# A planner's model of DMA: from one long hold of SyncE to a short issue and a turn on shared rings

## The chip, the cores and the metric

The kernel runs on one core of a Trainium2 chip. The metric is device time of one execution in microseconds (us): 921.68 us is the median of three runs before the change (920.78 to 922.54). A profile of one execution goes with it. TensorE is PE in its rows, with its weight loads as PEld; VectorE is DVE, ScalarE is ACT, GpSimd is POOL, SyncE is SP; SPq and ACTq are the queues on which SyncE and ScalarE issue DMAs.

## The reference

Attention with a threshold over 8 batches, 8 heads, 576 tokens and 64 dimensions a head, and behind it a gated convolutional feed-forward network, all float32:

```python
scores = scale * np.matmul(q, k.transpose(0, 1, 3, 2))
thresh = np.max(scores, axis=-1, keepdims=True) - tau
scores = np.where(scores >= thresh, scores, -1000000000.0)
scores = scores - np.max(scores, axis=-1, keepdims=True)
attn = np.exp(scores)
attn = attn / (np.sum(attn, axis=-1, keepdims=True) + 1e-09)
x = np.matmul(attn, v)      # heads side by side: 512 columns
h = np.maximum(x @ w_in, 0.0)                  # 512 -> 1024
conv_out = sum(conv_w[k] * hp[:, k:k + S, :] for k in range(3))
gate = 1.0 / (1.0 + np.exp(-conv_out))
out = h * gate @ w_out                          # 1024 -> 512
```

## The kernel before, in words

Each batch is cut into two chunks of query rows (256 and 320 of the 576), and each chunk is worked through for four pairs of heads. A **unit** is one tile of up to 128 query rows of one pair: the scores on PE (`ps_s`, line 571 in batch 0 and for the 64-row tile at the end of a batch, line 578 elsewhere), their maximum on DVE (L586), the exponential on ACT (L595), the mask on DVE (L598), small steps on `few` (L592, L615, L619, L622), and the division by the sum on POOL (L631). The masked weights `em` are turned by PE (`ps_t`, L690) and brought from PSUM into `eT` by ACT (L685). For 28 of the tiles the turning is done by DMA (function `cross`: a store of `parts` to `rows` at L663 and two transposing DMAs into `eT` at L668). When all tiles of a pair are turned, PE multiplies by V: first one step `mixed` on half blocks (L745), then four steps on whole ones (L754). The result `x` feeds the network: `mm1` (`ph`, L782), relu, three taps and gate on ACT and DVE (L797 to L819), a low half on POOL (L328), and `mm2` (`po`, L840), whose output goes out through `ot` (L847, L848).

In batches 1 to 7 keys and queries are split into a high and a low float32r half. `prep_k` loads `xk` (L521), scales it and takes the high half on ACT (L522, L523), takes the low half on POOL (L328), and then three DMAs from SBUF to SBUF put half-height pieces into `ks` (function `halves`, L511). `prep_q` does the same for a chunk's queries, with six such DMAs. `xk` has two buffers, which the 64-row tiles' keys (`k`, L485) use too, so that a batch's first `xk` load waits for PE to have read the second last `k` of the batch before.

Nothing of the order on the engines is written out by hand. The functions hand every operation to a planner (`Plan.op`) with its engine, a planned duration, what it reads and writes, and a rank less an `ahead`; `Plan.run` then steps through planned time, gives each free engine the ready operation of lowest rank, and emits the instructions in the order in which it picked them. On the chip each engine takes its own stream in that order, and a semaphore wait at its head holds all behind it. So a changed planned duration changes no work, only the order of the streams and, where an operation has a choice of engines (`other`: some steps on `few`, the division, low halves), the engine that does it. PE's rows fall in four kinds (`rows`, `cols`, `turn`, `full`, by how the 128x128 array is divided), with a planned cost for a change between kinds (`SWITCH`).

In the planner before, a DMA on SP holds SP for its whole planned transfer, 2.6 ns a column (`sp(n)`; half of that or 360 ns for the pieces of `halves`), and its data is there 2000 ns after that. The three first weight loads and the first keys, issued by ACT, hold ACT for 450 ns and have a latency of their own.

Of the kernel before, what the change touches and what calls it, by code (L numbers as in the profile page):

```python
# [22 lines left out]

LATENCY = {"pe": 210.0, "act": 145.0, "dve": 110.0, "pool": 75.0, "sp": 2000.0}

# [26 lines left out]
FAR = 3  # L52
EMS = 5

KEEP = {'rows': 2.304, 'cols': 1.613, 'turn': 3.226, 'full': 2.304}
# [30 lines left out]
class Plan:  # L86
# [12 lines left out]

    def op(self, engine, ns, fn, w=(), r=(), ahead=0.0, other=None, kind=None, late=0.0, port=False):  # L100
# [14 lines left out]
        for x in bufs:  # L115
            x.left += 1
        self.ops.append((((engine, ns), *(other or ())), self.rank - ahead, fn if other is not None else lambda e: fn(), before, bufs, kind, late, port))

    def run(self):
# [12 lines left out]
        live, turn = set(), {}  # L132
        last, port = "full", 0.0

# [20 lines left out]
        while events:  # L155
            t = events[0][0]
            while events and events[0][0] <= t:
                _, _, kind, x = heapq.heappop(events)
                if kind == "ready":
                    i, e = x  # L160
                    if taken[i] is None:
                        heapq.heappush(ready[e], (self.ops[i][1] + (0.0 if e == self.ops[i][0][0][0] else ALT), i))
                        if e == self.ops[i][0][0][0]:
                            load[e] += self.ops[i][0][0][1]
                elif kind == "release":
                    live.discard(x)
                    wake(x[0])
                elif kind == "done":
                    engine = taken[x]
                    for j in after[x]:  # L170
                        waits[j] -= 1
                        for e in came[j]:
                            late = 0.0 if e == engine == "pe" else LATENCY[engine] + self.ops[x][6] + (60.0 if e in ("pool", "pe") and e != engine else 0.0)
                            came[j][e] = max(came[j][e], t + late)
                        if not waits[j]:
                            offer(j)
                    for b in self.ops[x][4]:
                        b.left -= 1
                        if not b.left:
                            post(t + LATENCY[engine], "release", (b.tag, b.turn % b.bufs))  # L180
            for e in ready:
# [67 lines left out]
def tile_tau_attention_gated_ffn(  # L249
# [15 lines left out]
    P = 128  # L265
# [64 lines left out]

    def sp(n):
        return 2.6 * n

# [12 lines left out]
    def split(src, n, name, high, low, hr, lr, queue="sp"):  # L346
# [37 lines left out]
        if queue == "sp":  # L384
            op("sp", sp(2 * n), load, w=[hi, lo], ahead=w + AHEAD["load"])
        else:
            op("act", 450, load, w=[hi, lo], ahead=90, late=sp(2 * n) + LATENCY["sp"])
        op("act", act(n), f0, w=[a], r=[hi], ahead=w)
# [86 lines left out]
    def plain(b):  # L475
        return b == 0

    def prep_rows(i, b, p, o, w, tag):
# [5 lines left out]
        if i:  # L484
            op("sp", sp(S + D), lambda: nc.sync.dma_start(k[:], kp[b, p]), w=[(k, 0), (k, 1)], ahead=a + 2)  # L485
            op("sp", sp(2 * w), lambda: nc.sync.dma_start(q[:], qd[b, p, :, :, o:o + w]), w=[(q, 0), (q, 1)], ahead=a + 2)
        else:
            for j, on in enumerate((slice(0, CH), slice(CH, S + D))):
                op(
                    "act", 450, lambda on=on: nc.scalar.dma_start(k[:, on], kp[b, p, :, on]), w=[(k, j)], ahead=210 - 10 * j,  # L490
                    late=1500 + sp(CH) * (1 + j)
                )
                op(
                    "sp", sp(w) + 400, lambda j=j: nc.sync.dma_start(q[:, j], qd[b, p, :, j, o:o + w]), w=[(q, j)], ahead=210 - 10 * j
                )
        if w < P:
# [6 lines left out]
    def halves(dst, src, of, ahead):  # L503

        x, view, parts = src
        for part, head in of:
            j, half = part
            n = view.shape[-1]
            op(
                "sp", max(sp(n) / 2, 360),  # L510
                lambda j=j, half=half, head=head: nc.sync.dma_start(  # L511
                    dst[half * D:(half + 1) * D, j, :n].bitcast(F32), view[head * D:(head + 1) * D].bitcast(F32)
                ),
                w=[(dst, part)], r=[(x, parts[head])], ahead=ahead
            )

    def prep_k(b, p, ks):

        a = AHEAD["prep"]
        xk = plan.buf(wk, "xk", 2, [P, S + D], F32, f"xk_{b}_{p}")  # L520
        op("sp", sp(S), lambda: nc.sync.dma_start(xk[:, :S], kt[b, p]), w=[(xk, 0), (xk, 1)], ahead=a + 2)  # L521
        op("act", act(S), lambda: nc.scalar.activation(xk[:, :S], xk[:, :S], AF.Copy, scale=0.125), w=[(xk, 0), (xk, 1)], ahead=a)  # L522
# [8 lines left out]
    def prep_q(i, b, p, q1, q2):  # L531
# [3 lines left out]
        a = AHEAD["prep"]  # L535
        op("sp", sp(w), lambda: nc.sync.dma_start(xq[:], qt[b, p, :, o:o + w]), w=[(xq, 0)], ahead=a + 2)
        op("act", act(w), lambda: nc.scalar.activation(q1[:, 0], xq[:], AF.Copy), w=[(q1, (0, 0)), (q1, (0, 1))], r=[(xq, 0)], ahead=a)
# [104 lines left out]
    def crossed(i, t):  # L642
        c, p = pairs[i]
        return not plain(chunks[c].b) and p % 2 == 0 and t == order(i)[0]

    def cross(u, em, eT, off):
# [4 lines left out]
        for j in range(2):  # L651
# [9 lines left out]
            )  # L661
        op(
            "sp", sp(2 * S), lambda: nc.sync.dma_start(rows[:].rearrange("(q two) k -> q two k", two=2), parts[:]),  # L663
            w=[(rows, 0)], r=[(parts, 0), (parts, 1)], ahead=a
        )
        for j in range(2):
            def turn(j=j):
                nc.sync.dma_start_transpose(eT[:].bitcast(U16)[:, off // D + j], rows[j * P:(j + 1) * P, :])  # L668

            op("sp", 1350, turn, w=[(eT, (off, j))], r=[(rows, 0)], ahead=a, late=400)  # L670

# [159 lines left out]
    def mm2(m):  # L831
# [15 lines left out]
        op("act", act(DO, True), lambda: nc.scalar.activation(ot[:, :DO], po[:], AF.Copy), w=[(ot, 0)], r=[(po, 0)])  # L847
        op("sp", sp(DO), lambda: nc.sync.dma_start(tokens[m * P:(m + 1) * P, :], ot[:, :DO]), r=[(ot, 0)])  # L848

# [159 lines left out]
```

## Time and profile before

| | |
|---|---|
| median of three runs | 921.68 us (920.78 to 922.54) |
| the profiled execution | 923.11 us, of it 921.3 us span |
| instructions | 19164 |
| granted TensorE clock, mean | 0.992 |
| DVE, ACT, POOL busy | 767.0, 675.5, 600.6 us |
| moved by DMA | 137.02 MB, mean 149 GB/s |

The span runs from the first instruction to the last; times in rows are counted from its start. A row of a group gives the engine, the output and input tiles, the shape and the count, then the busy time and the mean of one in ns; behind the bar stands the idle time of the engine just before such instructions and what ended most of it. In the order of time a row gives the start, the length, and in square brackets the idle time before it with its releaser. Of the 1.8 us of the execution that lie around its span the profile shows nothing.

### The profile page before, as it was taken

How to read it: one execution, taken by the hardware profiler on the slowest of the kernel's cores; microseconds unless marked ns; L12 is line 12 of the kernel's file. 1: busy time of each engine (PE TensorE's matmuls, PEld its weight loads, DVE VectorE, ACT ScalarE, POOL GpSimd, SP SyncE). 2: the span in 40 equal slices, each digit the busy share in tenths (PEclk: the TensorE clock that was granted, in tenths of full speed). 3: DMA queues.
4: the chain of work that ended last, by engine and by line, in shares of the span. 5: the costliest groups of instructions: out<-in, count | busy, mean ns of one | idle time of the engine just before them, and what ended most of it. 6: DMA issues, size and time to landing. Idle time of an engine off the chain costs nothing. (4 is left out here: it accounts for less than half of the span.)

```text
span 921.3 us, 19164 instructions
## 1 busy us (share of the span) xinstructions
PE 880.3 (96%) x6056; PEld 706.7 (77%) x6056; DVE 767.0 (83%) x1859; ACT 675.5 (73%) x1455; POOL 600.6 (65%) x1043
## 2 busy tenths in 40 slices
PE   5888899998999999999999999999999999999998
PEld 2445668877788788888788787887778887887896
DVE  5987998978889889896989789896898878998543
ACT  5877787868778787787778687787767768787642
POOL 3664776857758677884767667685676748676422
PEclk9998999999999999999999999999999999999999
DMA  6644247467675576547665566556656377664000
GB/s 212 200 146 133 69 122 188 121 173 181 169 200 148 145 203 160 146 132 187 183 181 147 146 163 158 136 150 185 171 154 179 99 181 180 174 138 115 16 24 34
DMA packets 148260, 137.02 MB, mean 149 GB/s; under 512 B 85312, under 2 KB 116288, under 8 KB 148160
## 3 DMA queue, kind: packets, MB, share of 16 engines
q1 hardware_dynamic: 147296, 133.90, 54.4%
q10 hardware_dynamic: 864, 1.90, 0.6%
q8 instruction: 49, 0.80, 0.4%
q14 instruction: 51, 0.42, 0.2%
HBM read 58.88 MB, written 25.95 MB: 92 GB/s over the span
## 5 line engine op out<-in xcount | busy, mean ns | idle before, releaser
L631 POOL TENSOR_SCALAR em<-em,few 128x576 f32<-128x576 f32 x284 | 256.9, 912 | 35.2 <-DVE few L622 26.6
L595 ACT ACTIVATE em<-ps_s,few 128x576 f32<-128x576 f32 x288 | 209.7, 743 | 57.2 <-DVE few L586 53.3
L598 DVE SCALAR_TENSOR_TENSOR em<-ps_s,few,em 128x576 f32<-128x576 f32 x288 | 230.7, 812 | 25.0 <-ACT em L595 15.7
L782 PE MATMUL ph<-x,w1h 128*128 128x322 f32 (+1 forms) x1024 | 239.4, 305 | 2.9 <-ACT hp L797 2.8
L586 DVE TENSOR_REDUCE few<-ps_s 128x1 f32<-128x576 f32 x288 | 210.8, 749 | 35.5 <-PE ps_s L578 19.7
L685 ACT ACTIVATE eT<-ps_t 128x512 f32<-128x512 f32 (+2 forms) x360 | 169.7, 488 | 33.8 <-PE ps_t L690 31.6
L782 PEld LDWEIGHTS ph<-x,w1h 128*128 128x128 f32 x1024 | 174.3, 190 | 7.8 <-ACT hp L797 4.4
L690 PE MATMUL ps_t<-ident,em 128*128 128x128 f32 x1060 | 158.6, 279 | 11.2 <-POOL em L631 3.8
L578 PE MATMUL ps_s<-ks,q 128*128 128x288 f32 x896 | 155.2, 305 | 3.8 <-issue 1.0
L690 PEld LDWEIGHTS ps_t<-ident,em 128*128 128x128 f32 x1060 | 125.3, 142 | 39.6 <-POOL em L631 13.2
L782 PE MATMUL ph<-x,w1l 128*128 128x322 f32 (+1 forms) x512 | 151.3, 296 | 0.0
L578 PEld LDWEIGHTS ps_s<-ks,q 128*128 128x128 f32 x896 | 128.6, 188 | 21.1 <-issue 11.2
L328 POOL TENSOR_TENSOR gl<-t,gh 128x255 fp32r<-128x255 f32 (+9 forms) x192 | 121.0, 643 | 30.1 <-ACT gh L819 28.9
L754 PE MATMUL pa<-eT,v 128*64 128x320 f32 (+1 forms) x1024 | 133.1, 412 | 0.0
L840 PE MATMUL po<-w2h,gh 128*128 128x512 f32 x288 | 117.7, 409 | 2.4 <-ACT hp L797 2.4
L754 PEld LDWEIGHTS pa<-eT,v 128*64 128x64 f32 x1024 | 70.8, 138 | 59.1 <-issue 15.9
L840 PE MATMUL po<-w2l,gh 128*128 128x512 f32 x288 | 113.3, 393 | 0.0
L840 PE MATMUL po<-w2h,gl 128*128 128x512 f32 x288 | 113.1, 393 | 0.1
L804 DVE SCALAR_TENSOR_TENSOR t<-hp,cr 128x321 f32<-128x321 f32 (+1 forms) x128 | 85.3, 667 | 33.2 <-ACT hp L797 29.1
L782 PEld LDWEIGHTS ph<-x,w1l 128*128 128x128 f32 x512 | 96.9, 189 | 0.2
L811 ACT ACTIVATE t<-t,cm 128x321 f32<-128x321 f32 (+1 forms) x128 | 68.4, 536 | 25.2 <-DVE t L804 13.9
L809 DVE SCALAR_TENSOR_TENSOR t<-t,hp 128x321 f32<-128x321 f32 (+1 forms) x128 | 77.7, 607 | 10.6 <-ACT t L811 9.8
(82 smaller groups left out, 1109.2 us busy)
## 6 DMA issues: line engine op xcount, KB each, us to landing
q<-q SPq DMA_DIRECT2D x336, 64.0 KB, 2.1
v<-in_vc_dram SPq DMA_DIRECT2D x64, 288.0 KB, 3.6
rows<-parts SPq DMA_DIRECT2D x28, 576.0 KB, 3.7
k<-in_kp_dram SPq DMA_DIRECT2D x35, 320.0 KB, 3.5
out_dram<-ot SPq DMA_DIRECT2D x36, 256.0 KB, 2.3
xk<-in_kt_dram SPq DMA_DIRECT2D x28, 288.0 KB, 3.6
ks<-xk SPq DMA_DIRECT2D x56, 144.0 KB, 2.6
xq<-in_qt_dram SPq DMA_DIRECT2D x56, 128.0 KB, 2.4
```

The costliest lines, as they stand in the source:

```text
L328: engines[e].tensor_tensor(dst, x, y, op=ALU.subtract)
L578: nc.tensor.matmul(ps[:, c, :CH], lhsT=q[:, h, o:o + n], rhs=k[:, h, c * CH:(c + 1) * CH], start=(i == 0), stop=(i == 1))
L586: nc.vector.tensor_reduce(few[:rows, nm], ps[:rows, :, :CH], op=ALU.max, axis=mybir.AxisListType.XY, negate=True)
L595: nc.scalar.activation(view(), ps[:rows, :, :CH], AF.Exp, bias=few[:rows, nm])
L598: nc.vector.scalar_tensor_tensor(view(), ps[:rows, :, :CH], few[:rows, th], view(), op0=ALU.is_ge, op1=ALU.mult, accum_out=few[:rows, total])
L631: engines[e].tensor_scalar(sl, sl, by, to, op0=ALU.mult, op1=ALU.add)
L685: "act", act(w, True), lambda dst=dst, src=src: nc.scalar.activation(dst(), src(pt), AF.Copy),
L690: nc.tensor.transpose(out=pt[:, at:at + P], in_=em[:, int(b * P):int(b * P) + P], identity=ident[:])
L754: nc.tensor.matmul(pa[j * D:(j + 1) * D, :w], lhsT=vt[:, blk, :], rhs=eT[:, :w // D, blk, :], start=False, stop=(r == 3))
L782: nc.tensor.matmul(ph[:, :an], lhsT=w1[w][:, cb, fs], rhs=xs[cb][:, h, :an], start=(cb == 0 and i == 0), stop=(cb == NCB - 1 and i == 2))
L804: nc.vector.scalar_tensor_tensor(t[:, :kn], hp[:, k:kn + k], cr[:, j, f:f + 1], y, op0=ALU.mult, op1=ALU.add)
L840: nc.tensor.matmul(po[:], lhsT=x[:, f, at:at + P], rhs=w[:, f, :], start=(f == 0 and i == 0), stop=(f == NFB - 1 and i == 2))
```

## The change

Only what the planner believes of DMAs. A DMA holds its queue for an issue of 330, 460 or 560 ns. From 600 ns after the start of the issue it takes a turn on the rings, one after the other in the order of issue, for `rows * (n * 0.225 + 4) * 0.0737` ns (rows of n elements); 950 ns after its turn the data is there and the buffers it read are free. All DMAs, those of ACT too, go through a new helper `put`; the transposing ones hold SP for 1560 ns and the rings for 1785. `CROSS` names which of a pair's 128-row tiles are turned by DMA; with (1, 0) they are the same 28 as before. The 6517 operations that the planner gets are the same, with the same dependencies.

```diff
-LATENCY = {"pe": 210.0, "act": 145.0, "dve": 110.0, "pool": 75.0, "sp": 2000.0}
+LATENCY = {"pe": 210.0, "act": 145.0, "dve": 110.0, "pool": 75.0, "ring": 950.0}
...
-                            late = 0.0 if e == engine == "pe" else LATENCY[engine] + self.ops[x][6] + (60.0 if e in ("pool", "pe") and e != engine else 0.0)
+                            late = 0.0 if e == engine == "pe" else (LATENCY["ring"] if self.ops[x][8] else LATENCY[engine]) + self.ops[x][6] + (60.0 if e in ("pool", "pe") and e != engine else 0.0)
...
-                post(free[e], "done", pick)
+                if self.ops[pick][8]:
+                    ring = max(ring, t + 600.0) + self.ops[pick][8]
+                    post(ring, "done", pick)
+                else:
+                    post(free[e], "done", pick)
...
-    def sp(n):
-        return 2.6 * n
+    def put(n, fn, issue=460, rows=P, queue="sp", **kw):
+        op(queue, issue, fn, ring=rows * (n * 0.225 + 4) * 0.0737, **kw)
...
-            op("sp", sp(2 * n), load, w=[hi, lo], ahead=w + AHEAD["load"])
+            put(2 * n, load, issue=330, w=[hi, lo], ahead=w + AHEAD["load"])
...
-            op(
-                "sp", max(sp(n) / 2, 360),
-                lambda j=j, half=half, head=head: nc.sync.dma_start(
+            put(
+                n, lambda j=j, half=half, head=head: nc.sync.dma_start(
                     dst[half * D:(half + 1) * D, j, :n].bitcast(F32), view[head * D:(head + 1) * D].bitcast(F32)
-                ),
+                ), issue=560, rows=D,
...
-        op("sp", sp(S), lambda: nc.sync.dma_start(xk[:, :S], kt[b, p]), w=[(xk, 0), (xk, 1)], ahead=a + 2)
+        put(S, lambda: nc.sync.dma_start(xk[:, :S], kt[b, p]), w=[(xk, 0), (xk, 1)], ahead=a + 2)
...
-        op("sp", sp(NBLK * D), lambda: nc.sync.dma_start(vt[:], vc[b, p]), w=[(vt, 0)], ahead=AHEAD["prep"])
+        put(NBLK * D, lambda: nc.sync.dma_start(vt[:], vc[b, p]), w=[(vt, 0)], ahead=AHEAD["prep"])
...
-        return not plain(chunks[c].b) and p % 2 == 0 and t == order(i)[0]
+        return not plain(chunks[c].b) and t in [x for x in order(i) if TILES[x][1] == P][:CROSS[p % 2]]
...
-        op(
-            "sp", sp(2 * S), lambda: nc.sync.dma_start(rows[:].rearrange("(q two) k -> q two k", two=2), parts[:]),
-            w=[(rows, 0)], r=[(parts, 0), (parts, 1)], ahead=a
+        put(
+            864, lambda: nc.sync.dma_start(rows[:].rearrange("(q two) k -> q two k", two=2), parts[:]),
+            w=[(rows, 0)], r=[(parts, 0), (parts, 1)], ahead=a, late=-500
         )
...
-            op("sp", 1350, turn, w=[(eT, (off, j))], r=[(rows, 0)], ahead=a, late=400)
+            op("sp", 1560, turn, w=[(eT, (off, j))], r=[(rows, 0)], ahead=a, late=100, ring=1785)
```

Since the lines of the code shift by two at most places, L511 of before is L513 of the changed kernel, L521 is L523, L578 is L580, and so on.

The streams differ nearly everywhere, and mostly by a few places. The first place is SP at the start of batch 4, whose keys are `xk_4_0`, `xk_4_1` and `ks_4_0`, `ks_4_1` (batch, pair of heads); `q1_`, `q2_` are queries, `v_` values, `rows_`, `eT_` the turning by DMA, `ot_` the output. Before:

```order
L521 DMA xk_4_0_5476<-in_kt_dram 128x576
L511 DMA q1_32_5421<-q1_32_5421 64x256 x2
L511 DMA q2_32_5454<-q2_32_5454 64x256
L547 DMA v_30_5498<-in_vc_dram 128x576
L668 DMA_TRANSPOSE eT_30_5506<-rows_74_5423 128x9x128 x2
L547 DMA v_31_5558<-in_vc_dram 128x576
L511 DMA ks_4_0_5553<-ks_4_0_5553 64x576
L511 DMA ks_4_0_5553<-xk_4_0_5476 64x576
L511 DMA q1_32_5421<-q1_32_5421 64x256
L511 DMA q2_32_5454<-q2_32_5454 64x256
L521 DMA xk_4_1_5604<-in_kt_dram 128x576
L511 DMA ks_4_0_5553<-xk_4_0_5476 64x576
```

And in the changed kernel, on the same engine from the same load on:

```order
L523 DMA xk_4_0_5466<-in_kt_dram 128x576
L523 DMA xk_4_1_5471<-in_kt_dram 128x576
L493 DMA q_36_5476<-in_qd_dram 128x2x64
L493 DMA q_37_5482<-in_qd_dram 128x2x64
L549 DMA v_30_5509<-in_vc_dram 128x576
L670 DMA_TRANSPOSE eT_30_5517<-rows_74_5422 128x9x128 x2
L549 DMA v_31_5561<-in_vc_dram 128x576
L513 DMA ks_4_0_5526<-ks_4_0_5526 64x576
L513 DMA ks_4_0_5526<-xk_4_0_5466 64x576
L513 DMA ks_4_1_5577<-ks_4_1_5577 64x576
L513 DMA q1_33_5597<-q1_33_5597 64x256 x2
L513 DMA ks_4_0_5526<-xk_4_0_5466 64x576
```

The load of the second pair's keys, which had eleven DMAs between it and the first pair's, stands right behind it, and so do the loads `q_36`, `q_37` of the small tile's queries, which stood 20 places later; the last piece of `ks_4_0` stands behind the first piece of `ks_4_1`.

The second place is PE a little later in the same batch, where the scores `ps_s_80` are the first to use `ks_4_0`; `ph_6` is the network of an earlier chunk, `ps_t` the turning. Before:

```order
L690 MATMUL ps_t_78_4_5638<-ident_83,em_78_5528 128x128 x4
L782 MATMUL ph_6_0_5629<-x_26_4987,w1h_233 128x256
L782 MATMUL ph_6_0_5629<-x_26_4987,w1l_267 128x256
L782 MATMUL ph_6_0_5629<-x_26_4987,w1h_233 128x256
L782 MATMUL ph_6_0_5629<-x_27_5013,w1h_233 128x256
L782 MATMUL ph_6_0_5629<-x_27_5013,w1l_267 128x256
L782 MATMUL ph_6_0_5629<-x_27_5013,w1h_233 128x256
L690 MATMUL ps_t_79_0_5652<-ident_83,em_79_5574 128x128 x4
L690 MATMUL ps_t_79_4_5658<-ident_83,em_79_5574 128x128 x4
L782 MATMUL ph_6_1_5666<-x_24_4697,w1h_233 128x256
L782 MATMUL ph_6_1_5666<-x_24_4697,w1l_267 128x256
L782 MATMUL ph_6_1_5666<-x_24_4697,w1h_233 128x256
```

These rows end right ahead of `ps_s_80_0`. In the changed kernel PE has, from the same turning on:

```order
L692 MATMUL ps_t_78_4_5657<-ident_83,em_78_5551 128x128 x4
L580 MATMUL ps_s_80_0_5662<-ks_4_0_5526,q1_32_5385 128x288
L580 MATMUL ps_s_80_0_5662<-ks_4_0_5526,q2_32_5398 128x288
L580 MATMUL ps_s_80_0_5662<-ks_4_0_5526,q1_32_5385 128x288
L580 MATMUL ps_s_80_0_5662<-ks_4_0_5526,q2_32_5398 128x288
```

The eleven rows of `ph_6` and `ps_t_79` between the turning and the first use of `ks_4_0` (9 and 8 matmuls) now stand behind that use.

The third place is PE in batch 0, at the product with V of pair 2 (`pa_2`: one `mixed` step of line 745, then four steps of line 754), with the scores `ps_s_8` of a later tile. Before:

```order
L745 MATMUL pa_2_527<-eT_2_437,v_2_300 64x256 x2
L571 MATMUL ps_s_8_0_532<-k_4_383,q1_4_402 128x288 x2
L571 MATMUL ps_s_8_1_539<-k_4_383,q1_4_402 128x288 x2
L754 MATMUL pa_2_527<-eT_2_437,v_2_300 64x256 x8
L398 MATMUL pw_stage_4_560<-stage_4_f_487,ident_83 128x512
```

And in the changed kernel:

```order
L747 MATMUL pa_2_474<-eT_2_405,v_2_277 64x256 x2
L756 MATMUL pa_2_474<-eT_2_405,v_2_277 64x256 x8
L405 MATMUL pw_stage_3_500<-stage_3_f_364,ident_83 128x512
L406 MATMUL pw_stage_3_500<-w1h_275,minus_126 128x512
L692 MATMUL ps_t_6_0_530<-ident_83,em_6_431 128x128 x4
```

The scores no longer part the product's steps. Over the program 25 of the 36 `mixed` steps were followed at once by the steps of their own product, and now 34 are; the changes to and from the `rows` and `cols` kinds number 157 before and 142 after, 57 of them in the first 200 planned PE operations of either kernel.

More of the change, by code (lines that the diff above doesn't have):

```diff
@@ L98, in buf, with op @@
         return b
-    def op(self, engine, ns, fn, w=(), r=(), ahead=0.0, other=None, kind=None, late=0.0, port=False):
+    def op(self, engine, ns, fn, w=(), r=(), ahead=0.0, other=None, kind=None, late=0.0, port=False, ring=0.0):
         i = len(self.ops)
@@ L116, in op @@
             x.left += 1
-        self.ops.append((((engine, ns), *(other or ())), self.rank - ahead, fn if other is not None else lambda e: fn(), before, bufs, kind, late, port))
+        self.ops.append((((engine, ns), *(other or ())), self.rank - ahead, fn if other is not None else lambda e: fn(), before, bufs, kind, late, port, ring))
     def run(self):
@@ L384, in split @@
         if queue == "sp":
[L385 removed]
+            put(2 * n, load, issue=330, w=[hi, lo], ahead=w + AHEAD["load"])
         else:
[L387 removed]
+            put(2 * n, load, issue=330, queue="act", w=[hi, lo], ahead=90)
         op("act", act(n), f0, w=[a], r=[hi], ahead=w)
```

23 lines of the change are left out of this document (10 added, 13 removed).

## The prediction

> **What bounds the kernel now.** I read the page's busy times and clock first, then the stretches, then PE's rows in order of time for the idle time in them.
>
> ```profile
> span 921.3 us, 19164 instructions
> PE 880.3 (96%) x6056; PEld 706.7 (77%) x6056; DVE 767.0 (83%) x1859; ACT 675.5 (73%) x1455; POOL 600.6 (65%) x1043
> ```
>
> PE is the bound: 880.3 of 921.3 us, so 41.0 us of idle time is all that another order can win, apart from work that PE does less of. The stretches say where it lies (start and end, then busy time of PE, PEld, DVE, ACT, POOL, the granted clock, the DMA engines' share, GB/s):
>
> ```profile
> 0.00:50.00 50.00, 36.61 (x188) 19.37 (x190) 39.14 (x107) 32.82 (x66) 24.46 (x55) 0.97 0.61 190
> 50.00:100.00 50.00, 44.87 (x268) 26.39 (x265) 41.23 (x93) 38.93 (x79) 29.40 (x43) 0.93 0.42 128
> 100.00:150.00 50.00, 44.40 (x295) 34.77 (x294) 47.42 (x105) 40.91 (x86) 35.94 (x56) 0.97 0.54 133
> 150.00:200.00 50.00, 49.89 (x347) 41.22 (x347) 41.86 (x106) 36.76 (x80) 34.81 (x67) 1.00 0.57 157
> ...
> 200.00:250.00 50.00, 47.39 (x344) 37.23 (x343) 45.67 (x108) 39.12 (x84) 35.37 (x57) 1.00 0.66 170
> ```
>
> The first 150 us hold 13.4, 5.1 and 5.6 us of the 41.0; everything behind them holds 16.9. The DMA engines are little more than half busy. So transfers as such bound nothing; what counts is when a wanted one lands, and what an order puts in front of PE.
>
> **The change part by part.** It alters no instruction's work. It alters order, and I cost four effects of that.
>
> (1) Changes between PE's kinds. The rows of the chain that ended last (start, length) show the matmuls right behind a product with V and the same ones elsewhere:
>
> ```profile
> 738.90 4.46 PE pa L754 x32
> 743.36 0.58 PE ps_t L690 x4
> ...
> 788.94 3.60 PE pa L754 x32
> 792.54 1.25 PE ps_s L578 x8
> ...
> 805.27 1.07 PE ps_s L578 x8
> ...
> 809.21 0.59 PE pa L745 x8
> 809.80 1.26 PE ps_s L578 x8
> ...
> 817.77 0.44 PE ps_t L690 x4
> ```
>
> A change costs 0.58 - 0.44 = 0.14 us (turning) to 1.26 - 1.07 = 0.19 us (scores). The order has 157 of them before and 142 after, and the first 200 planned operations, where PE is not the bound, have 57 in either, so the 15 saved lie behind them. 15 x 0.14 to 0.19 = 2.1 to 2.9 us; I take **-2.3**, nearer the turning, which follows such a product more often. Nothing hides it: it is PE's own time in stretches where PE is over 97% busy.
>
> (2) Loads for a new batch that come too late. PE's rows with an idle time in brackets, and ACT's row behind the first of them:
>
> ```profile
> 226.18 0.39 PE L782 MATMUL ph<-x,w1h 128*128 128x256 f32 x1 [2.08 <-ACT hp L797]
> 441.01 0.76 PE L578 MATMUL ps_s<-ks,q 128*128 128x288 f32 x4 [0.89 <-DMA ks<-xk]
> 654.90 0.77 PE L578 MATMUL ps_s<-ks,q 128*128 128x288 f32 x4 [1.05 <-issue]
> ```
>
> ```profile
> 227.47 0.31 ACT L497 ACTIVATE q<-q 128x128 f32<-128x128 f32 x1 [1.34 <-DMA q<-in_qd_dram]
> ```
>
> 441.01 and 654.90 are the first uses of a batch's second pair of keys, whose load moves up to stand behind the first pair's (the front's SP rows for batch 4). At 226.18 PE waits for ACT. ACT's next gap there, 1.34 us, is for a small query load, which moves 12 to 20 places up SP. The sum is 0.89 + 1.05 + 1.34 = 3.28; with the loads 6 us and more earlier I take it all, **-3.3**. Bounds: nothing, if ACT or DVE is next late, and -4.0, with 2.08 for 1.34.
>
> (3) The first keys of a batch. Here the change works against PE. SP's rows in batch 4, then PE's first use of these keys, then issue to landing (KB each, median us):
>
> ```profile
> 413.66 0.68 SPq L521 DMA_DIRECT2D xk<-in_kt_dram  x1
> ...
> 417.04 3.41 SPq L668 DMA_TRANSPOSE eT<-rows  x2
> ...
> 423.50 0.47 SPq L511 DMA_DIRECT2D ks<-ks  x1
> ...
> 427.50 0.46 SPq L511 DMA_DIRECT2D ks<-xk  x1
> ```
>
> ```profile
> 431.77 1.22 PE L578 MATMUL ps_s<-ks,q 128*128 128x288 f32 x8
> ```
>
> ```profile
> xk<-in_kt_dram SPq DMA_DIRECT2D x28, 288.0 KB, 3.6
> ks<-xk SPq DMA_DIRECT2D x56, 144.0 KB, 2.6
> ```
>
> The last piece is issued at 427.50, lands at about 430.1, and is used at 431.77: 1.7 us to spare. In the new order the use moves ahead of 9 matmuls of `ph` and 8 of `ps_t`. Their lengths are in these rows:
>
> ```profile
> 695.21 0.87 PE ps_t L690 x8
> ...
> 713.93 1.34 PE ph L782 x9
> ```
>
> That is 2.2 us, so the use would be 0.5 us too early if the last piece leaves SP when it did. It may leave 2.0 us earlier (right behind its sister at 425.02 plus an issue: no loss), or 1.0 us later, since it now stands behind a piece that waits for ACT and behind two query pieces of about half a microsecond each (1.5 us lost). I take 0.5, the middle and the one that changes SP least, and the same in batches 2, 3 and 5 to 7, where the first use moves by 2 to 28 places of the plan: 6 x 0.5 = **+3.0**, bounds 0 and +9.0. Batch 1 I leave out: there the first use moves 7 places back. What waits behind such a stall is all of PE's stream, so nothing hides it.
>
> (4) Batch 0. PE's rows again:
>
> ```profile
> 43.09 0.65 PE L745 MATMUL pa<-eT,v 64*64 64x256 f32 x4 [0.58 <-ACT eT L685]
> 46.81 0.78 PE L571 MATMUL ps_s<-k,q 64*128 64x288 f32 x2 [3.07 <-ACT q L500]
> ```
>
> ```profile
> 25.03 1.95 PE L754 MATMUL pa<-eT,v 128*64 128x256 f32 x16
> ```
>
> PE had begun `pa_2`, then waited 3.07 us for the queries of `ps_s_8`, while the 16 ready matmuls of `pa_2`, 1.95 us long, stood behind (the front's third place). Now they stand ahead and fill that much: **-2.0**. Against it: DVE is busy for 39.1 of these 50 us and does no less work, so PE may just wait later (bound 0). For more: the gap may go entirely (-3.1). The weight pieces come a few places later in every stream; the network's first use of them stands at the same PE place, and I cost this at nothing, covered by the attention work put ahead; without that cover it is about one piece on PE, 0.5 to 1 us.
>
> The clock is the open item here. It is granted at 0.97, 0.93 and 0.97 in the first three stretches, 50 x (0.03 + 0.07 + 0.03) = 6.5 us of full speed, and at 1.00 behind 150 us even where PE pauses for 2.08 us. If the loss comes from the head's idle time, filling it returns a part. I put nothing in the sum and keep up to -4 us as a bound.
>
> The Trainium skill ("TensorE: Matmul & The Clock Gate", section "HAM oscillation — how this bites in real kernels") has it that only idle gaps of TensorE over some 3.4 us cost clock. No gap behind the start is that long here, so by it the sum would stay as it is and the bound of -4 would be empty; the row of 0.93 in a stretch whose waits are shorter than that speaks against it, and the row decides.
>
> DMA issues themselves, 774 on SP, are as many as before. The choice of an engine for a small step moves 7 limits and 7 guards more to DVE, each like this row's:
>
> ```profile
> L592 DVE TENSOR_SCALAR few<-few,ntau 128x1 f32<-128x1 f32 x163 | 30.8, 208 | 0.8
> ```
>
> That is 14 x 0.21 = 2.9 us of DVE, hidden under PE, which is 113 us busier over the span.
>
> The **sum**: -2.3 - 3.3 + 3.0 - 2.0 = -4.6 us. The profiled execution took 923.11 us, 1.4 us over the median of the three; from it 918.5, and by the median of the runs **917.1 us**.
>
> **The rivals.** *Late keys (slower).* The planner now believes that keys are there earlier than the rows say. For `xk` it plans 600 + 128 x (576 x 0.225 + 4) x 0.0737 + 950 = 2.8 us against 3.6, for a piece of `ks` 600 + 630 + 950 = 2.2 against 2.6: 1.2 us a batch over the two steps. Also its plan never lets SP stand in front of a wait, while the real one does:
>
> ```profile
> SPq L848 <- ACT ot L847: 91.6, 19, 24.3
> SPq L511 <- ACT q L537: 46.7, 21, 5.9
> ```
>
> That is 138 us in which whatever stands behind on SP waits too. With the upper price of 1.5 us and the same again at the second keys, six batches lose 6 x 3.0 = 18.0; without the -3.3 and the -2.0, and with the -2.3, that is +15.7, or 937. The milder form is the first keys alone at 1.5: 9.0 - 2.3 = +6.7, or 928.4. It is slower than now as soon as a batch loses over (2.3 + 3.3 + 2.0) / 6 = 1.3 us. For it: planned landings are short. Against it: the K loads themselves start earlier and two at a time.
>
> *Idle time only moves.* PE waits mostly for a unit's chain on DVE, ACT and POOL, and DVE is 83% busy. If each pause that goes comes back a few units on, and the saved changes of kind end as waits, the time stays at 921.7. For it: the streams meet again at the same sets of PE operations at many points, so gains in between must show as idle time somewhere. Against it: in the stretches behind 150 us PE has no such reserve of idle time.
>
> *The clock and the bursts too.* Earlier attention work leaves the network's matmuls as filler for DVE's crowded moments. Then of the 16.9 us of idle time behind 150 us another 4 go, with the clock's 4: 917.1 - 8 = 909.
>
> *The order is as before.* That the change does nothing is excluded by the front's rows.
>
> **How the numbers follow.** The forecast, a gain of 2 to 8 us, 0.45; clock and bursts 0.12; only moved 0.21; late keys 0.22. Faster by over 0.2% (below 919.8, about what a measurement of this kernel can tell from no change): nearly all of the first two, 0.57. Within 0.2%: 0.20. Slower: 0.23. The range leaves out one in ten on each side: down to 910, near the clock case, and up to 925, half way into the milder late keys. The forecast's own range is 913 to 920.
>
> **What would show it.** (1) Groups L690 and L578 on PE with a lower mean, PE's busy time 2 us lower. (2) Two `xk` loads back to back at each batch's start, and no PE gap of about 1 us at the second keys. (3) Gaps of 0.5 us, and not 1.5, at the first use of `ks` in batches 2 to 7. (4) The 3.07 us gap near 47 us down to about 1, with the clock of the first stretches as the open item. The prediction is wrong if PE's idle time stays near 41 us, or if PE gaps released by DMA or by ACT's `xk` rows sum to more than 8 us.

## The result, and the profile after

| | before | after |
|---|---|---|
| median of four runs each, taken side by side | 921.57 us (920.78 to 922.54) | 913.67 us (912.62 to 914.90) |
| ratio, 95% interval | | 0.9914 (0.9897 to 0.9932) |
| the profiled execution, of it span | 923.11, 921.3 us | 912.62, 910.8 us |
| granted TensorE clock, mean | 0.992 | 0.993 |

The change makes the kernel 7.9 us faster. The two profiled executions lie 10.5 us apart, because the one of before took longer than its median and the one of after is the shortest of its four. So differences between the two traces are about 2.6 us too large in sum. The span and PE's line on the page of after:

```profile
span 910.8 us, 19147 instructions
PE 874.6 (96%) x6056; PEld 708.6 (78%) x6056; DVE 751.2 (82%) x1871; ACT 673.8 (74%) x1459; POOL 603.5 (66%) x1027
```

PE is busy 5.7 us less than before (880.3) and idle for 36.2 us instead of 41.0. The stretches of after, with the columns of the prediction's:

```profile
0.00:50.00 50.00, 37.08 (x202) 20.37 (x202) 37.80 (x102) 33.77 (x69) 22.73 (x47) 1.00 0.60 194
50.00:100.00 50.00, 44.28 (x263) 27.23 (x264) 43.02 (x93) 38.29 (x78) 33.46 (x48) 0.93 0.41 128
100.00:150.00 50.00, 42.94 (x277) 32.14 (x277) 46.17 (x115) 40.55 (x85) 37.79 (x58) 0.93 0.54 146
150.00:200.00 50.00, 50.00 (x373) 41.86 (x374) 47.65 (x122) 40.36 (x90) 39.09 (x69) 1.00 0.60 152
200.00:250.00 50.00, 49.69 (x357) 41.07 (x350) 43.04 (x111) 40.46 (x84) 34.91 (x52) 1.00 0.79 198
```

The first 150 us now hold 12.9 + 5.7 + 7.1 = 25.7 us of idle time, 1.6 more than before. Behind them are 36.2 - 25.7 = 10.5, 6.4 less than before's 16.9. The difference of the two traces is therefore -5.7 (PE's busy time) + 1.6 (the first 150 us) - 6.4 (the rest) = -10.5 us. Nothing is won at the start, where most of the idle time is.

In batch 4 after the change, the loads of the first two pairs of keys, ACT's splitting of the second pair, the last piece of `ks_4_1`, and its first use on PE:

```profile
409.96 0.92 SPq L523 DMA_DIRECT2D xk<-in_kt_dram  x2
...
415.95 0.67 ACT L524 ACTIVATE xk<-xk 128x576 f32<-128x576 f32 x1
419.52 0.69 ACT L525 ACTIVATE ks<-xk 128x576 fp32r<-128x576 f32 x1
...
424.86 0.46 SPq L513 DMA_DIRECT2D ks<-xk  x1
...
432.53 0.77 PE L580 MATMUL ps_s<-ks,q 128*128 128x288 f32 x4
```

The gap of 0.89 us at this use (441.01 before) is gone, and the last piece starts on SP 7.7 us ahead of the use. ACT's two steps on the second pair stood much later before:

```profile
430.76 0.68 ACT L522 ACTIVATE xk<-xk 128x576 f32<-128x576 f32 x1
432.57 0.69 ACT L523 ACTIVATE ks<-xk 128x576 fp32r<-128x576 f32 x1
```

The load moved by 17 us (426.82 before), and ACT's second step by 13. Some 4 us of each is the trace's own lead at this place (the batch's first load leaves at 409.96 instead of 413.66). Which of the two moves matters is decided by the experiments `early_keys` and `late_keys`.

At the start, SP's second queries and the two loads of V, ACT's step on the first queries, and PE:

```profile
2.17 0.68 SPq L493 DMA_DIRECT2D q<-in_qd_dram  x1
2.90 1.48 SPq L549 DMA_DIRECT2D v<-in_vc_dram  x2
...
5.98 0.72 ACT L503 ACTIVATE q<-q 128x256 f32<-128x256 f32 x2 [2.82 <-DMA q<-in_qd_dram]
...
6.45 2.46 PE L573 MATMUL ps_s<-k,q 64*128 64x288 f32 x8 [6.45 <-ACT q L503]
...
52.14 1.33 PE L573 MATMUL ps_s<-k,q 64*128 64x288 f32 x4 [4.63 <-DVE em L600]
```

PE's first row before:

```profile
4.53 1.33 PE L571 MATMUL ps_s<-k,q 64*128 64x288 f32 x4 [4.53 <-ACT q L500]
```

PE starts at 6.45 us instead of 4.53. Three more loads are under way when the first queries come in, and ACT waits 2.82 us for queries. The gap of 3.07 us at 46.81 is gone, but a gap of 4.63 us, released by DVE, stands at 52.14. In the trace fifteen small steps on the convolution's weights (L454) hold DVE from 45.86 to 49.31, ahead of the maximum that this chain needs, and steps on a piece of the network's weights (L383, L386) hold it from 49.90 to 51.26, ahead of the mask.

### The profile page after: what moved, and what is told of

It is laid out like the page before. It is cut to its first block, busy times and chain, and to the rows that moved or that the text cites. A ratio compares the mean times of both kernels' runs of the same rounds, so it can differ in the third digit from the quotient of the medians.

```text
span 910.8 us, 19147 instructions
## 1 busy us (share of the span) xinstructions
PE 874.6 (96%) x6056; PEld 708.6 (78%) x6056; DVE 751.2 (82%) x1871; ACT 673.8 (74%) x1459; POOL 603.5 (66%) x1027
## 4 chain that ended last, share of the span: by engine, by line
PE 73%; ACT 8%; DVE 6%; POOL 5%; DMA 4%; issue 3%; SPq 2%; ACTq 0%; POOLq 0%; DVEq 0%
PE po L842 20%; PE ph L784 16%; PE pa L756 12%; PE ps_s L580 11%; PE ps_t L692 9%; PE ps_s L573 3%; ACT em L597 2%; POOL em L633 2%; DVE em L600 2%; ACT eT L687 2%; PE pa L747 2%; DVE few L588 2%; DMA q<-in_qd_dram 1%; SPq L513 1%; DMA q<-q 1%
## 5 line engine op out<-in xcount | busy, mean ns | idle before, releaser
L633 POOL TENSOR_SCALAR em<-em,few 128x576 f32<-128x576 f32 x287 | 262.8, 924 | 29.9 <-DVE few L624 22.1
L784 PE MATMUL ph<-x,w1h 128*128 128x322 f32 (+1 forms) x1024 | 233.7, 304 | 0.6 <-ACT hp L799 0.5
L580 PE MATMUL ps_s<-ks,q 128*128 128x288 f32 x896 | 156.8, 306 | 5.3 <-DMA q<-q 2.1
L580 PEld LDWEIGHTS ps_s<-ks,q 128*128 128x128 f32 x896 | 129.2, 189 | 20.2 <-issue 8.2
L806 DVE SCALAR_TENSOR_TENSOR t<-hp,cr 128x321 f32<-128x321 f32 (+1 forms) x128 | 75.6, 594 | 28.0 <-ACT hp L799 28.0
L813 ACT ACTIVATE t<-t,cm 128x321 f32<-128x321 f32 (+1 forms) x128 | 68.0, 535 | 25.2 <-DVE t L806 12.2
L811 DVE SCALAR_TENSOR_TENSOR t<-t,hp 128x321 f32<-128x321 f32 (+1 forms) x128 | 73.1, 573 | 11.4 <-ACT t L813 9.8
```

The source lines that it names most:

```text
L580: nc.tensor.matmul(ps[:, c, :CH], lhsT=q[:, h, o:o + n], rhs=k[:, h, c * CH:(c + 1) * CH], start=(i == 0), stop=(i == 1))
L633: engines[e].tensor_scalar(sl, sl, by, to, op0=ALU.mult, op1=ALU.add)
L784: nc.tensor.matmul(ph[:, :an], lhsT=w1[w][:, cb, fs], rhs=xs[cb][:, h, :an], start=(cb == 0 and i == 0), stop=(cb == NCB - 1 and i == 2))
L806: nc.vector.scalar_tensor_tensor(t[:, :kn], hp[:, k:kn + k], cr[:, j, f:f + 1], y, op0=ALU.mult, op1=ALU.add)
```

## The experiments

Three explanations were weighed. The first is that the gain is the forecast's terms: loads that come earlier, and fewer changes of kind on PE. The second is that it comes from one part of the new model, either the short issue or the rings, or from one part of the program. The third is that any new order moves the time by several us, and this one is a good draw. Three sets of four kernels were run, each beside runs of the kernel before. "Idle" is the span less PE's busy time on the page; "changes" are the planned changes of kind behind the first 200 planned PE operations. The runs of before spread from 920 to 928 us, most of them near the lower end; the ratio weighs all runs and can differ from the quotient of the medians by some 2 us.

| kernel | median (runs) | ratio, 95% interval | PE busy, idle | changes |
|---|---|---|---|---|
| before, the three sessions | 921.96, 921.94, 922.92 | 1 | 880.3, 41.0 | 100 |
| after, from the result | 913.67 (4) | 0.9914 (0.9897 to 0.9932) | 874.6, 36.2 | 85 |
| `ring_late` | 919.48 (8) | 0.9962 (0.9936 to 0.9988) | 877.4, 39.8 | 90 |
| `ring_early` | 928.12 (10) | 1.0047 (1.0028 to 1.0066) | 885.1, 43.3 | 100 |
| `long_hold` | 931.08 (5) | 1.0079 (1.0052 to 1.0106) | 885.2, 44.5 | 109 |
| `short_hold` | 942.12 (4) | 1.0198 (1.0159 to 1.0237) | 883.0, 57.8 | 93 |
| `old_1950` | 928.25 (5) | 1.0081 (1.0063 to 1.0099) | 880.9, 41.9 | 101 |
| `old_2050` | 921.67 (9) | 0.9993 (0.9977 to 1.0008) | 882.9, 37.3 | 105 |
| `new_925` | 920.33 (9) | 0.9976 (0.9955 to 0.9998) | 876.8, 40.7 | 86 |
| `new_975` | 922.33 (9) | 0.9990 (0.9971 to 1.0009) | 879.5, 41.4 | 99 |
| `new_again` | 915.16 (6) | 0.9910 (0.9883 to 0.9937) | 874.9, 40.9 | 85 |
| `early_keys` | 921.73 (12) | 0.9990 (0.9970 to 1.0009) | 882.2, 38.9 | 100 |
| `late_keys` | 960.60 (6) | 1.0400 (1.0368 to 1.0431) | 882.7, 76.0 | 85 |
| `old_start` | 920.23 (12) | 0.9971 (0.9954 to 0.9989) | 872.6, 43.6 | 85 |

### One part of the program, one part of the model

`ring_late` plans with the old model through batch 0 and with the new one from the loads of batch 1 on; `ring_early` is the other way round (`rank < 17`). The transposing DMAs follow the same switch.

```diff
+RINGS = lambda rank: rank >= 17
...
-        op(queue, issue, fn, ring=rows * (n * 0.225 + 4) * 0.0737, **kw)
+        if RINGS(plan.rank):
+            op(queue, issue, fn, ring=rows * (n * 0.225 + 4) * 0.0737, **kw)
+        elif queue == "sp":
+            kw.pop("late", 0)
+            op("sp", old or max(2.6 * n * rows / P, floor), fn, **kw)
+        else:
+            op("act", 450, fn, late=slow, **kw)
```

> The planner's old model of DMA for everything up to batch 0, the new one from the loads of batch 1 on. Theory A (the gain lies behind batch 0, where the idle time of PE went from 12.3 to 4.6 us and its own work from 757.3 to 752.7 us): 911 to 915 us, with the first matmul back at about 4.5 us. Theory B (the gain is made in the first hundred us, by the reordered start): 919 to 922. Theory C (any reshuffling of the streams moves the time by several us either way): anything from 912 to 925.

> The new model up to batch 0, the old one from the loads of batch 1 on. Theory A: 919 to 923 us, no faster than before. Theory B: 912 to 916. Theory C: anything from 912 to 925.

In the third and the fourth kernel the whole program has one half of the new model. `long_hold` holds SP as long as before, and the data comes by the rings. `short_hold` has the short issue, and the data comes when the old model says, without rings.

```diff
+        hold = old or max(2.6 * n * rows / P, floor)
+        op(queue, hold if queue == "sp" else issue, fn, ring=rows * (n * 0.225 + 4) * 0.0737, **kw)
```

```diff
+        if queue == "sp":
+            hold = old or max(2.6 * n * rows / P, floor)
+            op("sp", issue, fn, late=hold - issue, **kw)
+        else:
+            op("act", 450, fn, late=slow, **kw)
```

> SP held for the whole planned transfer as before, but the data there by the rings' turn and 950 ns. Theory A in its form A1 (what counts is that SP is planned free at once, so that a batch's loads stand back to back): 919 to 924 us. In its form A2 (what counts is the earlier planned landing, which puts attention ahead): 912 to 916.

> SP held for the issue alone as in the change, but the data there when the old model had it (hold and 2000 ns), no rings. A1: 912 to 916 us. A2: 919 to 923.

By the medians, the new model behind batch 0 alone wins 2.5 us, and in batch 0 alone it loses 6.2 (3.5 and 4.3 by the ratios). Together they win 7.9, so the parts do not add. The halves of the model add even less: one half costs 9.1 us, the other 20.2, and both together win 7.9. That batch 0 gains nothing fits the stretches above. No single part can be given the gain; what made `short_hold` as slow as it is was not looked into further.

### A constant that means nothing to the chip

A planned latency was moved by 25 or 50 ns (2.5%), in the old model and in the new one. No operation or dependency changes on the chip, only the order and, with it, the engine of a few small steps (DVE has 1871 instructions in after and 1877 in `new_925`). The other three kernels differ in the number alone.

```diff
-LATENCY = {"pe": 210.0, "act": 145.0, "dve": 110.0, "pool": 75.0, "ring": 950.0}
+LATENCY = {"pe": 210.0, "act": 145.0, "dve": 110.0, "pool": 75.0, "ring": 925.0}
```

> The changed kernel with 925 ns after the rings' turn in place of 950; PE operations 0.7 places from the change, 143 changes of kind against 142. A: 912 to 916. C: farther off.

> The same with 975 ns: PE operations 3.0 places from the change, and 161 changes of kind against 142, as many as before the change. A: 912 to 917. If the saved changes of kind are most of PE's 4.6 us less work: 2 to 3 us above the change, 916 to 918. C: anything from 912 to 925.

> The kernel before with the planned latency of a DMA at 1950 ns in place of 2000. It means nothing for the machine and moves a PE operation by 2.1 places in the mean. If a reshuffling alone moves the time (theory C), by several us: below 918 or above 925. If the model counts (A): 919.5 to 923.5.

> The same with 2050 ns; PE operations 2.3 places from before. C: below 918 or above 925. A: 919.5 to 923.5.

The third explanation holds to a large part. 25 ns in either direction take back 6 and 8 of the 8 us, and 50 ns off the old constant cost 6.3, while 50 ns on top of it change nothing that can be told (0.9993). The three orders of the new model have medians of 913.7, 920.3 and 922.3 (mean 918.8), the three of the old one 921.6, 928.3 and 921.7 (mean 923.8). With some 8 us between orders of one model, the 5.0 us between the means are suggested by three orders each, not shown.

### The same order, with one thing moved

For the last four kernels the order on every engine was written into the kernel as a list, so that one engine's stream could be changed while the others stand as they were:

```diff
     def run(self):
+        raw = zlib.decompress(base64.b64decode(STREAMS))
         n = len(self.ops)
...
+        for at in range(n):
+            i = raw[2 * at] + 256 * raw[2 * at + 1]
...
+            self.ops[i][2](("pool", "act", "sp", "dve", "pe")[raw[2 * n + at]])
```

**`new_again`** is the order of after, unchanged.

> The changed kernel's order, instruction for instruction, written out as a list instead of planned; nothing differs on the chip. It tells how much of 913.7 us belongs to the order and how much to the session in which it was timed. Both theories expect 913.7, within 1.5 us; PE idle behind planned operation 200 of 4 to 6 us. 917 or more would mean that the gain of 8 us was itself partly a draw of the session, and that the other orders' differences of 6 to 9 us from it are read too large.

The median is 915.16, and the ratio, 0.991, is that of the first measurement (0.9914): the gain belongs to the order, not to a session. Its profiled execution is the longest of its six, 917.55 us with 915.8 us of span. Step by step against the trace of after, which has the same streams, PE is 0.3 us late at 352 us and 4.5 us late at 443, and from there to the end between 4.0 and 5.0. In that stretch SP, ACT and PE have:

```profile
384.44 0.59 SPq L493 DMA_DIRECT2D q<-in_qd_dram  x1
...
388.51 0.31 ACT L500 ACTIVATE q<-q 128x128 f32<-128x128 f32 x1 [2.17 <-DMA q<-in_qd_dram]
...
391.75 0.41 PE L784 MATMUL ph<-x,w1h 128*128 128x322 f32 x1 [0.80 <-ACT hp L799]
393.60 0.77 PE L580 MATMUL ps_s<-ks,q 128*128 128x288 f32 x4 [0.70 <-DVE few L594]
```

and the trace of after, for the same transfer and the same step:

```profile
381.72 0.59 SPq L493 DMA_DIRECT2D q<-in_qd_dram  x1
...
384.63 0.31 ACT L500 ACTIVATE q<-q 128x128 f32<-128x128 f32 x1
```

In one execution the queries are there 2.3 us after the end of their issue and ACT does not wait; in the other ACT waits 2.17 us for them, until 3.5 us after it, and two gaps on PE follow. The load itself also leaves 2.7 us later in the second, with PE 1.6 us late at that place. So two executions of one order differ by up to 5 us, and a difference of a few us between single traces proves nothing.

**`early_keys`** has the order of before, with three of SP's DMAs moved up in batches 2 to 7; in batch 4:

```diff
 L521 DMA xk_4_0<-in_kt_dram
+L521 DMA xk_4_1<-in_kt_dram
+L486 DMA q_36<-in_qd_dram
+L486 DMA q_37<-in_qd_dram
 L511 DMA q1_32<-q1_32
...
-L521 DMA xk_4_1<-in_kt_dram
```

> The old order on every engine, instruction for instruction, but in batches 2 to 7 SP's load of the second pair of keys and the two small query loads behind it stand right behind the load of the first pair, as in the new order. Loads theory (term 2 of the forecast): the gaps at 441.01 (0.89), 654.90 (1.05) and 226.18 (1.34 of 2.08) go, 921.6 - 3.3 = 918.3 us, PE idle behind operation 200 from 12.3 to about 9. Order theory (time comes out of hundreds of small differences in the order, and no single place carries it): the gaps close, but PE waits the same time a few operations on, 920.5 to 922, idle 11 to 13.

```profile
414.65 1.37 SPq L521 DMA_DIRECT2D xk<-in_kt_dram  x2
...
431.49 0.68 ACT L522 ACTIVATE xk<-xk 128x576 f32<-128x576 f32 x1
433.29 0.70 ACT L523 ACTIVATE ks<-xk 128x576 fp32r<-128x576 f32 x1
...
441.55 0.77 PE L578 MATMUL ps_s<-ks,q 128*128 128x288 f32 x4 [0.63 <-DMA ks<-xk]
...
654.99 0.77 PE L578 MATMUL ps_s<-ks,q 128*128 128x288 f32 x4 [1.03 <-issue]
```

The load leaves 11 us earlier than before, yet ACT comes to the second pair of keys at its old place (431.49; 430.76 before), and PE's gaps stay: 0.63 for 0.89, and 1.03 for 1.05. The gap of 2.08 us at 226.18 stays as well (2.01 at 228.99), though ACT's wait for the small queries there is gone. The time is 1.2 us below before's, with an interval from 2.8 faster to 0.8 slower: not the 3.3 us of the loads theory. The order theory had the gaps close and come back later; they did not close. The profiled trace lies 3.0 us behind that of before at 140 us and 0.2 ahead of it at the end, so some 3 us of small waits may well have gone in this one execution, in places other than those named; the medians do not bear out as much.

**`late_keys`** is the reverse. It has the order of after, but in batches 2, 3, 5 and 7 SP's load of the second pair stands behind the last of the three pieces of the first pair's `ks`.

```diff
 L523 DMA xk_3_0<-in_kt_dram
-L523 DMA xk_3_1<-in_kt_dram
...
 L513 DMA ks_3_0<-xk_3_0
+L523 DMA xk_3_1<-in_kt_dram
```

> The new order on every engine, but in batches 2, 3, 5 and 7 SP's load of the second pair of keys moves back behind the first exchange of the first pair's last half, 4 to 8 places down SP. Loads theory: two to four gaps of 0.9 to 1.3 us return at the first use of the second pair, 916 to 918 us, PE idle behind operation 200 from 4.6 to 7 or 9. Order theory: 913.7 to 915, idle 4.6 to 6, since PE's and the other engines' orders, which carry the gain, are kept.

Both theories missed by over 40 us. ACT's waits by cause (total us, times, longest), then SP, ACT and PE in batch 3:

```profile
ACT xk L524 <- DMA xk<-in_kt_dram: 44.7, 10, 10.5
```

```profile
323.14 0.51 SPq L513 DMA_DIRECT2D ks<-ks  x1
...
324.33 3.02 SPq L670 DMA_TRANSPOSE eT<-rows  x2
...
328.07 1.15 SPq L513 DMA_DIRECT2D ks<-xk  x2
329.28 0.58 SPq L523 DMA_DIRECT2D xk<-in_kt_dram  x1
...
333.55 0.68 ACT L524 ACTIVATE xk<-xk 128x576 f32<-128x576 f32 x1 [10.43 <-DMA xk<-in_kt_dram]
...
335.19 1.94 PE L692 MATMUL ps_t<-ident,em 128*128 128x128 f32 x8 [10.04 <-ACT eT L687]
```

In the new order ACT takes the second pair right behind the first. With the load nine places down, SP reaches it only after pieces that wait for ACT and POOL themselves and after 3.02 us of transposing DMAs. ACT then stands 10.43 us at the head of its stream, and the copies into `eT` for which PE waits stand behind it. Step by step against the trace of after, PE falls behind by 10.8, 12.2, 10.7 and 11.1 us in the four batches, 44.8 in sum; the medians of `late_keys` and `new_again` lie 45.4 apart. Part of it is clock: behind each of the four pauses the clock's records stand at half for 10.24 us, and PE is busy 882.7 us instead of 874.9 with the same stream.

These two kernels answer what the load is worth. Moved up alone it wins nothing that the medians can tell (0.9990, 0.9970 to 1.0009); the new order on ACT without it, in four batches, costs 45 us. The new plan moves both, and in batch 4 the gap at the second keys closes with ACT getting to them 13 us earlier, which the early load permits. No run moves the load and ACT's steps together and nothing else, so what the pair is worth stays open.

**`old_start`** has the order of after, but SP's first seven transfers as before:

```diff
+L374 DMA stage_3<-in_w_in_dram
 L493 DMA q1_1<-in_qd_dram
 L549 DMA v_0<-in_vc_dram
 L549 DMA v_1<-in_vc_dram
-L374 DMA stage_3<-in_w_in_dram
```

> The new order on every engine, but SP's first seven transfers stand as before: the stage load, then the queries, then the two loads of V. The first matmul moves from 6.45 back to about 4.5 us. If PE carries a late start to the end, 913.7 - 1.9 = 911.8 us; if the waits of batch 0 (stages through ACT and DVE) take it up, 913 to 914.5. A slower run, over 915, would mean that the loads of V, now later, are wanted in batch 0.

```profile
3.63 0.33 SPq L374 DMA_DIRECT2D stage<-in_w_in_dram  x1
5.16 0.69 SPq L493 DMA_DIRECT2D q<-in_qd_dram  x1
...
13.39 0.72 ACT L503 ACTIVATE q<-q 128x256 f32<-128x256 f32 x2 [7.82 <-DMA q<-in_qd_dram]
...
4.65 1.33 PE L573 MATMUL ps_s<-k,q 64*128 64x288 f32 x4 [4.65 <-ACT q L503]
...
15.74 1.81 PE L573 MATMUL ps_s<-k,q 64*128 64x288 f32 x6 [6.69 <-DVE em L600]
```

PE starts at 4.65 us, and the whole gains nothing: its second tile comes 5.1 us later than in after (15.74 for 10.67), and the median is 5.1 us above `new_again`. The queries of the second tile leave at 5.16 us instead of 2.17, because SP first stands before the stage load until 3.63, and ACT waits 7.82 us for them with the exponentials behind it. The place that decides is that of the queries, not of V, which none of the three expected outcomes had. In the old order ACT does the exponentials ahead of those queries (at 6.70 and 9.37 us in the trace of before), and with the same seven transfers it waits only 0.34 us for them there (at 13.45). So the order of after needs these queries early and starts 1.9 us later for it; whether an order could have both, no run tells.

## Why the prediction was right, point by point

The time, 913.67 us, lies in the range and just inside the forecast's own (913 to 920); the sign was right. The sum was too small by 3.3 us (-4.6 for -7.9), and of its four terms only the second came out near its size, in part for another reason. The agreement is in part luck: the two orders 25 ns away, at 920.3 and 922.3, lie outside the forecast's 913 to 920, and nothing in the sum tells them from this one. By one of the prediction's own signs, PE's idle time staying near 41 us, this order comes out right in one execution and wrong in another: 36.2 us in after, and 40.9 in `new_again`, where nearly all of the gain is PE's busy time.

**(1) Changes of kind, -2.3: too large a price, and a test that could not show it.** By medians from start to start of consecutive PE steps, over both traces behind operation 200, a step on whole blocks of 256 columns takes 0.432 us before another of its kind (196 times) and 0.532 before a `full` one (22 times). `mm1` takes 0.355 before its own kind (364 times) and 0.442 before `rows` (12 times). So a change costs 0.09 to 0.10 us and 15 of them 1.4 to 1.5, not 2.1 to 2.9; the lengths of rows that the forecast used overlap their neighbours. For the same reason the means by line, named as the test, did not fall:

```profile
L692 PE MATMUL ps_t<-ident,em 128*128 128x128 f32 x1060 | 157.8, 280 | 6.5 <-POOL em L633 5.1
L580 PE MATMUL ps_s<-ks,q 128*128 128x288 f32 x896 | 156.8, 306 | 5.3 <-DMA q<-q 2.1
```

```profile
L690 PE MATMUL ps_t<-ident,em 128*128 128x128 f32 x1060 | 158.6, 279 | 11.2 <-POOL em L631 3.8
L578 PE MATMUL ps_s<-ks,q 128*128 128x288 f32 x896 | 155.2, 305 | 3.8 <-issue 1.0
```

The first two rows are after's, the last two before's. PE's busy time did fall, by 5.7 us in the profiled execution and by 5.4 in `new_again`, more than 15 such prices. Among the orders of the table without long stalls, those with 85 or 86 changes have 872.6 to 876.8 us of it, that with 90 has 877.4, and those with 99 to 105 have 879.5 to 885.1. That goes together. A part is the clock: PE is busy at half clock for 24.2 us in before, 22.1 in after and 17.6 in `new_again` (the start phase and the drops of the last section), and half of that time is lost, so by an estimate from these times 1.0 of the 5.7 us and 3.3 of the 5.4 are clock. What else makes up the rest is open.

**(2) Late loads, -3.3: right in what would go, wrong in why.** The gaps at the second keys are gone, and with others they make the 6.4 us less of idle time behind 150 us (3.4 in the longer execution of `new_again`: 40.9 less 27.4 in its first 150 us leaves 13.5). But the step that read "the loads come too late" fell: moved alone, they leave the gaps (`early_keys`). At 441.01 the row that ends the wait, `ks<-xk`, is the exchange behind ACT and POOL, and ACT's turn to split the keys set it. At 654.90 the wait was not for keys at all: the last piece had left SP at 648.18, and the row names no transfer. DVE's mask on earlier scores ends at 654.79, 0.11 us before PE starts:

```profile
653.97 0.82 DVE L598 SCALAR_TENSOR_TENSOR em<-ps_s,few,em 128x576 f32<-128x576 f32 x1 [1.63 <-ACT em L595]
```

In `early_keys` the two are 0.10 us apart (654.89 and 654.99). That the mask frees the scores' buffer for PE is likely, not shown. So 1.05 of the 3.28 us stood in the wrong term.

**(3) First keys, +3.0: it did not happen.** In after the last piece of `ks_b_0` starts on SP 3.2 to 4.9 us ahead of its first use in batches 2 to 7, and the only gap there is 0.27 us. The forecast took the piece's time on SP as in before, while ACT's work on these keys had moved up with the use. It is the same omission as in (2).

**(4) Batch 0, -2.0: taken back on the spot, as its bound of 0 had it.** The 3.07 us gap went, and DVE's 4.63 us gap came. The start that is 1.9 us later was not in the sum at all. Nor did the clock return: 1.00, 0.93 and 0.93 in the first three stretches is a loss of 50 x 0.14 = 7.0 us, for 6.5 before; by the clock's own records (last section) it is 6.8 in both.

**The rivals.** *Late keys* did not come about, though `late_keys` shows the mechanism at its full price, at ACT rather than at PE: 45 us in four batches, 11 us each, where one load comes later than the other streams were ordered for. *Idle time only moves* held for batch 0 and not behind it. *Clock and bursts* had the right place for one of its two halves, idle time behind 150 us; its other half, the clock, gave nothing. None of the cases said that a step of 25 ns in one planned constant is worth as much as the change.

## What to carry to other kernels

When a planner's order moves as a whole, a wait that ends with a transfer need not be set by the load: look for the first in-order engine behind it that has its turn late, and ask whether that turn moves too. Moving one queue's instruction alone can bring nothing in one order and cost 45 us in another, so the streams of SP and ACT have to be moved together. Before a planner's model is called better, shift one of its constants by a few per cent and time that as well; here three of four such steps moved the time by 6 to 9 us, as much as the change itself.

## What the runs showed of the hardware that was not expected

**The clock after a pause.** Granted clock is the third column from the right, in after and then in before:

```profile
47.00:52.00 5.00, 0.50 (x6) 0.05 (x2) 4.76 (x17) 1.89 (x4) 1.51 (x3) 0.91 0.57 196
52.00:57.00 5.00, 4.86 (x14) 2.90 (x15) 4.32 (x10) 3.15 (x7) 2.88 (x4) 0.50 0.51 143
```

```profile
47.00:52.00 5.00, 5.00 (x25) 2.53 (x25) 3.44 (x9) 1.02 (x3) 2.99 (x4) 0.67 0.28 105
```

Behind the gap of 4.63 us the clock is granted at 0.50 for five us, and behind the gap of 3.07 us in before at 0.67. The clock's records in the kept traces hold 1.0 and 0.5 alone, in stretches that are whole multiples of 3.41 us. At 0.5 stand 46.92 to 50.34, 74.23 to 81.06 and 111.78 to 115.19 us in before, 51.10 to 57.93 and 105.72 to 112.54 in after: 13.7 us in either, which is 6.8 us of full speed. No long gap is needed. Here are PE's rows of before around 74.23, and the stretch that holds them (columns as above):

```profile
72.98 0.76 PE L571 MATMUL ps_s<-k,q 64*128 64x288 f32 x4 [1.44 <-DVE em L598]
74.25 1.56 PE L745 MATMUL pa<-eT,v 64*64 64x320 f32 x4 [0.51 <-ACT eT L685]
...
70.00:80.00 10.00, 8.05 (x27) 3.72 (x24) 7.93 (x18) 5.59 (x13) 4.91 (x8) 0.71 0.47 155
```

In the 3.41 us ahead of 74.23 PE is busy for 1.5 us, in pieces, and no gap is longer than 1.44. Cut into steps of 3.41 us from the clock's first record on, all 14 kept traces show the same: ahead of each of the 39 drops PE is busy for at most 1.84 us of the step, ahead of every step that stays at full clock for at least 1.65, and full clock comes back only behind a step with 3.25 us or more. So what costs clock here is a step of which PE fills about half or less, however the idle time is cut up. The Trainium skill ("TensorE: Matmul & The Clock Gate", section "HAM oscillation — how this bites in real kernels") puts the limit at idle gaps of some 3.4 us; the 4.63 us agree with it, the 3.07 and the 1.44 us do not.

**The slow phase at the start is in no row of the clock.** Four matmuls of the same shape at the same place of the same stream, in before and then in `early_keys`, whose batch 0 is unchanged:

```profile
20.20 0.76 PE L571 MATMUL ps_s<-k,q 64*128 64x288 f32 x4 [0.44 <-DVE em L598]
```

```profile
20.39 1.33 PE L571 MATMUL ps_s<-k,q 64*128 64x288 f32 x4 [0.43 <-DVE em L598]
...
26.97 0.76 PE L571 MATMUL ps_s<-k,q 64*128 64x288 f32 x4
```

They take 1.33 us until PE has become fast, and 0.76 from then on until the first drop above, while the granted clock of these stretches reads 1.00 in both traces. The view has nothing to read there: the trace's first record of the clock, at 1.0, begins at 19.62 us in the one execution and at 25.87 in the other, where the lengths change. By 58 us the second is 2.7 us late, nearly all of it from these steps. The Trainium skill ("TensorE: Matmul & The Clock Gate", section "What's actually happening") has the clock's window run freely, so that this point varies by 0.5 us either way; here two executions are 6.2 us apart, with PE busy for only 4.5 and 4.0 of the 8 us from 4 to 12 us.
